# Two GpSimd multiplications in place of a compare and a ScalarE absolute value, in the weight preparation of an attention and two-layer kernel

## The chip, the cores and the metric

The kernel runs on one core of one Trainium2 chip. The time is the device time of one execution in microseconds; the time before is the median of three runs. The profile is of one further execution of the same program.

## The reference

The inputs are q, k, v (4 batches, 8 heads, 576 positions, 64 columns), s (4, 8, 576) and four weight matrices that arrive as float64: `w_in` 512x2048 and `w_out` 2048x512 for each of two layers.

```
scores = q k^T / 8 + min(-(cum_i - cum_j), 0), causal     cum = cumsum(max(s, 0))
attn   = softmax(scores);  x = attn v   -> 2304 tokens x 512
layer 1: h = x @ w_in;  g = h * clip(h + 3, 0, 6) / 6;  x = g @ w_out
layer 2: h = x @ w_in;  g = h * sigmoid(h);             out = g @ w_out
```

All results are float32.

## The kernel before

One core does everything. Each matrix product runs with operands split into a high and a low part (three matmuls for one product), so weights and activations each exist as two fp32r tiles.

**Weights.** A weight chunk is 128 rows of 512 float64 numbers, loaded as 1024 32-bit words per row, so the low and the high words lie alternately, 8 bytes apart. `Chunk` (L130 to L187) makes float32 numbers of them by integer steps. `load` issues the DMA on SP's queue. `fields` (L151 to L164) makes three tiles of words: ScalarE (ACT) scales the low words in place (L159); ACT writes `mag`, the absolute value of the high words, taken as float32, times 2^-112 (L160); GpSimd (POOL) overwrites the high words by the sign bit as an integer, from "less than zero" times -2^31 (L161). `join` puts them together on VectorE (DVE): `mag` shifted left by 3 or'ed with the sign words (L172), plus the low words (L176). Then `high` copies the result as fp32r on ACT (L120) and `low` subtracts on the DVE (L187). The tile `mag` comes from a pool of three, so that a chunk's `mag` can be written when the chunk three before it has been read.

There are 64 chunks: 16 of `i` (from `w_in`) and 16 of `o` (from `w_out`) for each layer. `Feed.tick` runs one step of this line of work: `high` of the chunk two behind, `fields` of the current one, `join` of the one behind, `low` of the chunk two behind, and the load of the chunk three ahead. The first layer's 32 chunks are ticked from the opening on; the second layer's `o` chunks are ticked, and its `i` chunks are made in pairs by `Two` (L887 on), beside the last steps of layer 1 and the first steps of layer 2. `Two.join` calls `fields` for both chunks of a pair and then `join`; `sums` and `split` (L915, L925, L927) make seven combinations of quarters from them, which go through DRAM.

**Order of work.** `slot` (L734 on) writes the order out by hand: in one slot stand one attention head's scores and exponentials, the transposes and the product with v of the head before, at most one step of layer 1 (`first`, `gate_high`, `second`, `gate_low`), and some ticks of the weight feed. Nine slots have no step of layer 1, the others have one. After the heads, layer 1 runs on its last block with the second layer's weights beside it, and then layer 2 (`step2`) on three blocks of 768 tokens. Each engine works through its own stream in order; an instruction that waits holds up all behind it on its engine. Waits are set where tiles are written and read. The framework orders the streams before the run by its own estimate of time.

POOL's other work: memsets of two rows of each new head (L407, L408, before SP loads the head), copies of the gate `g` to `gh` (L114 by `pool_copy`, two scalars, multiply and multiply), the softmax scaling of later heads (L551), the low part of v (L476).

Of the kernel before, what the change touches and what calls it, by code (L numbers as in the profile page):

```python
# [13 lines left out]
AF = mybir.ActivationFunctionType  # L14
ALU = mybir.AluOpType
# [4 lines left out]
SIGN = -(2**31)  # L20


def f32(ap):
    return ap.bitcast(F32)
# [3 lines left out]
def kernel(  # L28
# [15 lines left out]
    nc = tc.nc  # L44
# [43 lines left out]
    def heads_of(x):  # L88
# [8 lines left out]
        out=cmask[:, NZ:], in_=cmask[:, NZ:], pattern=[[-1, P]],  # L97
# [32 lines left out]
    class Chunk:  # L130
# [20 lines left out]
        def fields(self):  # L151

            self.mag = stage.tile([P, DM], I32, tag="mag", name=f"mag{self.nm}")
            if self.src.dtype == F32:
                nc.scalar.copy(f32(self.mag), self.val)
                self.val = f32(self.mag)
                return
            low, high = self.words
            nc.scalar.activation(low, low.bitcast(U32), AF.Copy, scale=2.0**-29)  # L159
            nc.scalar.activation(f32(self.mag), f32(high), AF.Abs, scale=2.0**-112)  # L160
            nc.gpsimd.tensor_scalar(  # L161
                out=high, in0=f32(high), scalar1=0.0, scalar2=float(SIGN),
                op0=ALU.is_lt, op1=ALU.mult,
            )  # L164

        def join(self):
# [166 lines left out]
    def bank(kind, shape, name):  # L333
# [11 lines left out]
        out=srow, in0=srow, scalar1=0.0, scalar2=1.0 / SCALE, op0=ALU.max, op1=ALU.mult  # L345
# [876 lines left out]
```

## Time and profile before

| what | value |
|---|---|
| median of three runs | 1017.48 us (1015.5 to 1018.98) |
| the profiled execution | 1021.31 us, of which span 1019.5 us |
| busy in the span: PE, DVE, ACT, POOL | 97%, 70%, 51%, 33% |
| chain that ended last, by engine | PE 78%, DVE 12%, ACT 3%, DMA 2%, POOL 2%, issue 2% |
| mean granted TensorE clock | 0.991 of full speed |

The page adds up each engine's busy time over one execution. An engine's busy share is a mean over stages: attention with the first layer's weights (to about 150 us), attention with layer 1 (to about 525), the last block of layer 1 with the second layer's weights and the turn to layer 2 (to about 650), layer 2. A DVE or POOL instruction that is held back by another engine while it runs counts as busy all that time. Wait rows name the waiting instruction, its releaser, the sum, the times and the longest.

### The profile page before, as it was taken

How to read it: one execution, taken by the hardware profiler on the slowest of the kernel's cores; microseconds unless marked ns; L12 is line 12 of the kernel's file. 1: busy time of each engine (PE TensorE's matmuls, PEld its weight loads, DVE VectorE, ACT ScalarE, POOL GpSimd, SP SyncE). 2: the span in 40 equal slices, each digit the busy share in tenths (PEclk: the TensorE clock that was granted, in tenths of full speed). 3: DMA queues.
4: the chain of work that ended last, by engine and by line, in shares of the span. 5: the costliest groups of instructions: out<-in, count | busy, mean ns of one | idle time of the engine just before them, and what ended most of it. 6: DMA issues, size and time to landing. Idle time of an engine off the chain costs nothing.

```text
span 1019.5 us, 18411 instructions
## 1 busy us (share of the span) xinstructions
PE 989.4 (97%) x6404; PEld 912.1 (89%) x6404; DVE 715.0 (70%) x1724; ACT 521.3 (51%) x1144; POOL 340.5 (33%) x446
## 2 busy tenths in 40 slices
PE   8988989999999999999999999899999999999997
PEld 5788989999999999999998887789988999888996
DVE  5798998878778888887737799867574334743343
ACT  5798655555556566566526565546353232532232
POOL 7376754453245444444415366423000000000000
PEclk9998999999999999999999999999999999999999
DMA  4686112212312322322114965443354341432411
GB/s 153 197 286 225 38 37 83 74 57 59 91 57 65 92 58 68 94 59 67 59 42 136 380 247 175 146 186 114 145 189 165 132 144 74 177 137 110 145 73 62
DMA packets 52068, 124.80 MB, mean 122 GB/s; under 512 B 10004, under 2 KB 31752, under 8 KB 48648
## 3 DMA queue, kind: packets, MB, share of 16 engines
q1 hardware_dynamic: 51528, 122.97, 35.6%
q8 instruction: 51, 0.84, 0.3%
q10 hardware_dynamic: 448, 0.66, 0.2%
q14 instruction: 41, 0.34, 0.1%
HBM read 98.96 MB, written 24.63 MB: 121 GB/s over the span
## 4 chain that ended last, share of the span: by engine, by line
PE 78%; DVE 12%; ACT 3%; DMA 2%; POOL 2%; issue 2%; DVEq 0%; POOLq 0%; ACTq 0%; SPq 0%
PE a L1029 6%; PE a L1030 6%; PE a L1031 6%; PE h L1013 5%; PE h L1014 5%; PE h L1015 5%; PE acc L300 5%; PE ph L260 5%; PE acc L301 5%; PE acc L299 5%; PE ph L262 5%; PE ph L261 5%; PE poB L617 4%; PE pt0B L567 1%; DVE mago L172 1%
## 5 line engine op out<-in xcount | busy, mean ns | idle before, releaser
L300 PE MATMUL acc<-gl,wo 128*128 128x256 f32 (+1 forms) x512 | 155.0, 304 | 2.7 <-DVE gl L280 2.7
L260 PE MATMUL ph<-xh,wi 128*128 128x256 f32 (+1 forms) x512 | 152.8, 299 | 3.4 <-DVE g L273 3.4
L301 PE MATMUL acc<-gh,wo 128*128 128x256 f32 (+1 forms) x512 | 152.7, 300 | 0.0
L262 PE MATMUL ph<-xh,wi 128*128 128x256 f32 (+1 forms) x512 | 151.3, 296 | 0.6 <-DVE wi L187 0.6
L261 PE MATMUL ph<-xl,wi 128*128 128x256 f32 (+1 forms) x512 | 150.9, 295 | 0.0
L299 PE MATMUL acc<-gh,wo 128*128 128x256 f32 (+1 forms) x512 | 145.2, 301 | 3.1 <-DVE gh L122 3.1
L1071 ACT ACTIVATE gh<-h 128x384 fp32r<-128x384 f32 x96 | 50.3, 524 | 187.7 <-DVE h L1079 187.6
L1029 PE MATMUL a<-wo,gh 128*128 128x512 f32 x288 | 113.5, 394 | 2.6 <-ACT gh L1071 2.5
L1030 PE MATMUL a<-wo,gh 128*128 128x512 f32 x288 | 113.5, 394 | 0.0
L300 PEld LDWEIGHTS acc<-gl,wo 128*128 128x128 f32 x512 | 97.9, 191 | 8.1 <-DVE gl L280 4.9
L260 PEld LDWEIGHTS ph<-xh,wi 128*128 128x128 f32 x512 | 97.0, 190 | 7.1 <-DVE g L273 2.3
L299 PEld LDWEIGHTS acc<-gh,wo 128*128 128x128 f32 x512 | 96.4, 191 | 7.1 <-ACT magi L160 2.5
L301 PEld LDWEIGHTS acc<-gh,wo 128*128 128x128 f32 x512 | 97.9, 191 | 3.6
L262 PEld LDWEIGHTS ph<-xh,wi 128*128 128x128 f32 x512 | 97.0, 189 | 3.8 <-DVE wi L187 0.8
L261 PEld LDWEIGHTS ph<-xl,wi 128*128 128x128 f32 x512 | 96.9, 189 | 2.9
L161 POOL TENSOR_SCALAR rawi<-rawi 128x512 int32<-128x512 f32 x32 | 68.8, 2150 | 76.9 <-ACT magi L160 57.1
L1031 PE MATMUL a<-wo,gl 128*128 128x512 f32 x288 | 90.0, 393 | 0.3 <-DVE gl L1073 0.3
L161 POOL TENSOR_SCALAR rawo<-rawo 128x512 int32<-128x512 f32 x32 | 69.5, 2176 | 44.2 <-ACT mago L160 41.1
L1073 DVE TENSOR_TENSOR gl<-h,gh 128x384 fp32r<-128x384 f32 x96 | 53.6, 558 | 40.7 <-ACT h L1072 39.1
L1079 DVE TENSOR_TENSOR h<-h,u 128x384 f32<-128x384 f32 x72 | 40.1, 557 | 54.8 <-PE h L1015 54.6
L273 DVE SCALAR_TENSOR_TENSOR g<-g,ph 128x512 f32<-128x512 f32 (+1 forms) x76 | 49.5, 652 | 34.5 <-ACT g L272 34.3
L272 ACT ACTIVATE g<-ph,half 128x512 f32<-128x512 f32 (+1 forms) x76 | 50.3, 662 | 37.9 <-PE ph L262 37.2
(232 smaller groups left out, 2655.8 us busy)
## 6 DMA issues: line engine op xcount, KB each, us to landing
w<-w_d SPq DMA_DIRECT2D x18, 1792.0 KB
w_d<-w SPq DMA_DIRECT2D x8, 1792.0 KB
k2B<-in_kT_dram SPq DMA_DIRECT2D x64, 144.0 KB
rawi<-in_w1i_dram SPq DMA_DIRECT2D x16, 512.0 KB
rawo<-in_w1o_dram SPq DMA_DIRECT2D x16, 512.0 KB
rawi<-in_w2i_dram SPq DMA_DIRECT2D x16, 512.0 KB
rawo<-in_w2o_dram SPq DMA_DIRECT2D x16, 512.0 KB
q2B<-in_qT_dram SPq DMA_DIRECT2D x64, 80.0 KB
```

Source lines behind the costliest of these rows:

```text
L161: nc.gpsimd.tensor_scalar(out=high, in0=f32(high), scalar1=0.0, scalar2=float(SIGN), op0=ALU.is_lt, op1=ALU.mult,)
L260: nc.tensor.matmul(o, wih[:, cs], xh[c], start=c == 0, stop=False)
L261: nc.tensor.matmul(o, wih[:, cs], xl[c], start=False, stop=False)
L262: nc.tensor.matmul(o, wil[:, cs], xh[c], start=False, stop=c == NDC - 1)
L299: nc.tensor.matmul(a, woh[:, cs], gh[:, jj, :], start=b0, stop=False)
L300: nc.tensor.matmul(a, woh[:, cs], gl[:, jj, :], start=False, stop=False)
L301: nc.tensor.matmul(a, wol[:, cs], gh[:, jj, :], start=False, stop=b1)
L1013: nc.tensor.matmul(ps, w[:, 0, cs], xh[:, c, :], start=c == 0, stop=False)
L1029: nc.tensor.matmul(accs[t], gh[:, k, cs], woh, start=b0, stop=False)
L1030: nc.tensor.matmul(accs[t], gh[:, k, cs], wol, start=False, stop=False)
L1031: nc.tensor.matmul(accs[t], gl[:, k, cs], woh, start=False, stop=b1)
L1073: nc.vector.tensor_tensor(out=gl[:, i, o], in0=g, in1=f32(gh[:, i, o]), op=ALU.subtract)
```

## The change

In `fields`, ACT's absolute value is gone. POOL makes `mag` as the high words, taken as float32, times 2^-112 and times 1.0, with their sign, and then overwrites the high words, as float32, by themselves times 0.0 and times 1.0: a zero that keeps the sign bit. The shift by 3 in `join` moves the sign bit of `mag` out, so that the or sets it from the sign words as before. The kernel is otherwise the same.

```diff
             nc.scalar.activation(low, low.bitcast(U32), AF.Copy, scale=2.0**-29)
-            nc.scalar.activation(f32(self.mag), f32(high), AF.Abs, scale=2.0**-112)
             nc.gpsimd.tensor_scalar(
-                out=high, in0=f32(high), scalar1=0.0, scalar2=float(SIGN),
-                op0=ALU.is_lt, op1=ALU.mult,
+                out=f32(self.mag), in0=f32(high), scalar1=2.0**-112, scalar2=1.0,
+                op0=ALU.mult, op1=ALU.mult,
+            )
+            nc.gpsimd.tensor_scalar(
+                out=f32(high), in0=f32(high), scalar1=0.0, scalar2=1.0,
+                op0=ALU.mult, op1=ALU.mult,
             )
```

## Rows read from the trace of the kernel before

**Rows 1.** The page: busy us, share of the span and instructions of each engine.
```profile
PE 989.4 (97%) x6404; PEld 912.1 (89%) x6404; DVE 715.0 (70%) x1724; ACT 521.3 (51%) x1144; POOL 340.5 (33%) x446
```

**Rows 2.** Busy us of each engine by stretch (from, to, length; then busy and instructions).
```profile
50.00:150.00 100.00, 88.02 (x676) 84.44 (x675) 94.18 (x236) 74.64 (x176) 69.51 (x54) 0.95 0.46 152
150.00:525.00 375.00, 375.00 (x3098) 371.72 (x3097) 297.61 (x886) 208.35 (x501) 157.82 (x289) 1.00 0.24 70
550.00:650.00 100.00, 95.39 (x408) 76.41 (x407) 89.95 (x136) 60.80 (x101) 59.33 (x35) 0.98 0.69 246
```

**Rows 3.** The same view for line L161 on POOL alone.
```profile
50.00:150.00 100.00, 54.35 (x25) 0.95 0.46 152
550.00:650.00 100.00, 45.36 (x21) 0.98 0.69 246
```

**Rows 4.** Who waited for whom, PE, 50 to 150 us (sum, times, longest).
```profile
PE acc L299 <- DVE gh L122: 3.1, 2, 2.3
```

**Rows 5.** Groups of ACT instructions, whole span (count | busy us, mean ns | idle before).
```profile
L160 ACT ACTIVATE mago<-rawo 128x512 f32<-128x512 f32 x32 | 21.4, 672 | 6.5 <-DVE wo L187 4.9 <-DVE w L927 1.0 <-DVE wi L187 0.5
L120 ACT CAST wo<-mago 128x512 fp32r<-128x512 f32 x32 | 19.9, 620 | 15.9 <-DVE mago L176 15.4 <-DVE sums L545 0.3
```

**Rows 6.** The chain that ended last, in order of time, opening (start us, us).
```profile
24.16 0.66 ACT mago L160
```

**Rows 7.** The same chain at 571 us.
```profile
571.66 0.55 ACT magi L160
572.35 1.98 POOL rawi L161
```

**Rows 8.** Instructions by line on POOL: duration ns, minimum, median, maximum.
```profile
L161 POOL TENSOR_SCALAR rawi<-rawi x32: 1967/2074/2747, 13.6 to 712.1; 128x512 int32<-128x512 f32 x32
L114 POOL TENSOR_SCALAR gh<-g x68: 608/622/1646, 100.0 to 624.7; 128x512 fp32r<-128x512 f32 x68
```

**Rows 9.** Who waited for whom, POOL, whole span.
```profile
POOL rawi L161 <- ACT magi L160: 57.1, 16, 8.6
```

**Rows 10.** Who waited for whom, DVE, 50 to 150 us.
```profile
DVE wi L187 <- ACT wi L120: 1.5, 2, 0.8
...
DVE magi L172 <- POOL rawi L161: 1.2, 1, 1.2
```

**Rows 11.** Timeline of POOL at 100 us (start us, us, instruction).
```profile
100.01 0.62 POOL L114 TENSOR_SCALAR gh<-g 128x512 fp32r<-128x512 f32 x1
100.59 0.84 POOL L114 TENSOR_SCALAR qaA<-q2A 64x256 fp32r<-64x256 f32 x1
101.40 2.00 POOL L161 TENSOR_SCALAR rawo<-rawo 128x512 int32<-128x512 f32 x1
```

**Rows 12.** Timeline of the DVE at 100 us.
```profile
100.08 1.09 DVE L172 SCALAR_TENSOR_TENSOR magi<-magi,rawi 128x512 int32<-128x512 int32 x1 [1.16 <-POOL rawi L161]
101.09 1.50 DVE L187 TENSOR_TENSOR wo<-mago,wo 128x512 fp32r<-128x512 f32 x1
```

**Rows 13.** Timeline of POOL at 60 us.
```profile
60.17 2.02 POOL L161 TENSOR_SCALAR rawi<-rawi 128x512 int32<-128x512 f32 x1 [0.83 <-ACT magi L160]
```

**Rows 14.** Timeline of the DVE at 61 us.
```profile
61.01 0.68 DVE L172 SCALAR_TENSOR_TENSOR mago<-mago,rawo 128x512 int32<-128x512 int32 x1
```

**Rows 15.** Groups of DVE instructions, 50 to 150 us.
```profile
L172 DVE SCALAR_TENSOR_TENSOR magi<-magi,rawi 128x512 int32<-128x512 int32 x13 | 10.5, 808 | 1.2 <-POOL rawi L161 1.2
L187 DVE TENSOR_TENSOR wi<-magi,wi 128x512 fp32r<-128x512 f32 x13 | 10.2, 783 | 1.5 <-ACT wi L120 1.5
L187 DVE TENSOR_TENSOR wo<-mago,wo 128x512 fp32r<-128x512 f32 x13 | 10.0, 771 | 0.0
L172 DVE SCALAR_TENSOR_TENSOR mago<-mago,rawo 128x512 int32<-128x512 int32 x13 | 9.5, 727 | 0.0
L176 DVE CUSTOM_DVE_ANT_0 magi<-rawi,magi 128x1024 uint16<-128x1024 uint16 x13 | 9.1, 703 | 0.1
L176 DVE CUSTOM_DVE_ANT_0 mago<-rawo,mago 128x1024 uint16<-128x1024 uint16 x12 | 9.0, 754 | 0.0
```

## The prediction

> **What bounds the kernel now.** I read the page's busy line first, then the busy time by stage, then who waits for whom in the two stages where TensorE is not full, then single instructions there.
>
> TensorE (PE) is busy 97% of the span [rows 1], so at most some 30 us could go. By stages [rows 2], PE is full from 150 to 525 us and nothing done to GpSimd (POOL) or ScalarE (ACT) there can count; the changed lines don't run there anyway. The open places are 50 to 150 us, where PE is busy 88.0 of 100 us, and 550 to 650 us, where it is busy 95.4 of 100: 12.0 and 4.6 us. In these two stages lie 25 and 21 of the 64 sign instructions of L161 [rows 3], since the weight chunks of the first and the second layer are being made ready. The engine that is nearly full beside PE is VectorE (DVE): 94.2 and 90.0 us of 100. In the first stage the DVE idles 5.8 us in all, and PE's longest stop there is for a DVE copy, 2.3 us [rows 4]. So between 50 and 150 us the in-order stream of the DVE sets the pace: what makes the DVE's work longer delays PE almost one for one, and what makes ACT or POOL quicker helps only where the DVE stands still for them.
>
> **The change part by part.**
>
> *ACT's absolute value (L160) goes.* 64 instructions of 0.67 us, 43 us [rows 5], but on an engine that is not the bound. Off the path this is worth nothing. It is on the path in a few places: once in the opening (24.16 us, 0.66 us, [rows 6]), which I take as 0.7 us gained, and three times between 571 and 593 us, where the chain goes through L160 into L161 (0.55, 0.55 and 0.68 us; [rows 7] is the first of the three, the others, at 581.29 and 592.09, repeat it).
>
> *POOL's compare (L161) becomes two multiplications.* Today one takes, for the chunks of `i`, 1.97 to 2.75 us, median 2.07 [rows 8]; those of `o` differ little. No POOL multiplication over words that lie 8 bytes apart is in the trace. The nearest rows: below, the same two-scalar multiplication over a dense 128x512 tile, median 0.62 us [rows 8]; above, L161 itself, the same strided words under another operation and an integer output, 2.07 us. For ACT the stride costs 0.05 us (0.67 for L160 against 0.62 for the dense cast of the same size, [rows 5]). I therefore stay near the lower end, 0.7 us each, so 1.4 us a chunk for 2.07. Alone this takes about 0.6 us from the latency of a chunk; with L160's share, each of the three places of the chain gets 1.15 to 1.28 us shorter, 3.5 us together.
>
> *The wait moves.* ACT's L160 stood for the chunk to land and for the `mag` tile three chunks back to be read (L187); now the first POOL multiplication stands for both. Behind it on POOL are the memsets of the next head (for which SP's loads wait), the gate copies L114 and the scalings L551. But POOL already stood there for the same events by way of ACT: 57.1 us before the chunks of `i` alone [rows 9]. So I cost this at nothing; if POOL's cover went, it would be the late `gh` copy, one instruction of 0.6 us.
>
> *Where the DVE stands still.* Between 50 and 150 us it waits 1.5 us for ACT (L120 behind L160 in ACT's queue) and 1.2 us for L161 [rows 10]. I let all of it go: 2.7 us.
>
> *What the second POOL instruction does to the DVE.* This is the term that decides. At 100.08 us the DVE instruction L172, which reads two tiles in SBUF, takes 1.09 us; a POOL copy of 0.62 us had started at 100.01. The next, L187, meets the start of two further POOL instructions and takes 1.50 us [rows 11, 12]; left alone, such an instruction takes 0.68 [rows 14]. So the start of a POOL instruction that reads SBUF holds back the DVE's two-tile instruction by about 0.41 us. The sign instruction does the same, but only in its beginning: L161 runs from 60.17 to 62.19, and L172, started 0.84 us into it, takes 0.68 us [rows 13, 14]. What counts is thus the number of POOL instructions, not their length, and the change doubles that number.
>
> The Trainium skill says it otherwise ("SBUF — State Buffer", "Who interferes with whom"): the pair of ports that the two engines share is taken for the whole instruction by whoever comes first, and the other blocks fully. The trace agrees that both are held up, but not with "the whole instruction": by that rule L172 of rows 14 would have waited until 62.19. By it, two instructions of 0.7 us would hold the DVE less than one of 2.07; that result stands among the rivals.
>
> The price of one: the upper end is 0.41 us, at every POOL instruction. The lower end is zero (the DVE happens to be at an instruction that reads PSUM or one tile); a gain is excluded, because the first multiplication starts where the compare did and the dense POOL copy of rows 11 holds the DVE like L161. As a mean: the weight instructions L172, L187 and L176 between 50 and 150 us [rows 15] exceed their usual 0.68 us by 13 x (0.128 + 0.103 + 0.091 + 0.047 + 0.023) + 12 x 0.074 = 6.0 us, over 25 L161 and 7 copies L114 of that size, 0.19 us each. Other two-tile instructions of the DVE are left out of this, so I take 0.25 us.
>
> **The sum.** 50 to 150 us: 25 x 0.25 = 6.3 us more DVE work, less 2.7 us of waits, +3.6. 550 to 650 us: 21 x 0.25 x 0.9 (the DVE's busy share there) = 4.7, less 3.5, +1.2. Opening: -0.7. Together +4.1 us. The profiled execution took 1021.3 us (span 1019.5 and 1.8 around it), 3.8 us above the median of the runs, 1017.5; the difference is added to the median: 1021.6, forecast 1021.5. With the mean stall at 0.41 it is 7.6 + 4.2 - 0.7 = +11.1 us (1028.6); with none, -2.7 - 3.5 - 0.7 = -6.9 us (1010.6). The sum crosses zero at a stall of 6.9 / (25 + 18.9) = 0.16 us. This crossing lies close under my 0.19 to 0.25, which is why the chances are spread.
>
> **Rivals.**
>
> *The shorter chain wins (not slower).* The second POOL instruction starts while the DVE is at work on a PSUM tile or still blocked by the first, so that its own price is under 0.16 us; then the waits for ACT and POOL that go decide. For it: L161 often ran beside L524 and small instructions without loss, as in rows 14. Against: the two follow each other on POOL at once, and in rows 11 and 12 each of three POOL instructions in a row took its share. Time: 1011, at a stall of zero.
> By the rule of the skill, the first figure to change would be the hold of a chunk, 2.07 to 1.4 us, and the gain would be limited only by PE's idle time in both stages, 16.6 us: 1001. Rows 14 speak against it; I give it 2%.
>
> *The stride is what makes L161 slow.* Then each multiplication costs 2.07 us. POOL's 69.5 us between 50 and 150 [rows 2] lose 54.4 [rows 3] and gain 25 x 4.14: 118.6 us of work in 100, +18.6 us; between 550 and 650 it is 100.9, +0.9, and the three places of the chain get 1.6 us longer each, +4.8: in all 24 us, 1041.5. For it: nothing in the trace separates stride from operation on POOL. Against: ACT pays 0.05 us for the same words, and L161 lets go of the DVE early, as if its reading were quick and its arithmetic slow. Between the ends, at 1.2 us each, POOL would be at 75 us of 100 in the first stage and the DVE would still decide: that lies in my range.
>
> *Nothing shows.* Both effects are absorbed: 1017.5. For it: the terms are a few us of opposite sign.
>
> **How the numbers follow.** About 0.3% (3 us) is what a measurement of this kernel can tell from no change. Chances: the forecast 52%, of which 33 end slower and 19 within 0.3%, since +4.1 is little more than 3; the shorter chain 24%, 20 of it faster and 4 within; the skill's rule 2%, faster; the stride 10%, slower; nothing shows 12%, of which 10 within and 2 faster. Faster 24%, within 33%, slower 43%. The range is 1011 to 1029: from a stall of zero to one at every instruction. It leaves out the stride and the skill's rule, and some of the ends. The forecast's own range is 1017 to 1027.
>
> **What would show it.** The two new POOL groups at 0.62 to 0.9 us each where the DVE doesn't hold them; at 2 us the stride is right. L172, L176 and L187 between 50 and 150 us at means some 0.1 us higher, the DVE at over 97 us of that 100, and PE idle there more than 12 us; if the means stay and PE idles less, the shorter chain was right. Between 571 and 593 us, 1.3 to 1.5 us from the landed chunk's turn on POOL to L172. The prediction is wrong if the DVE's means don't rise, or if they do and PE doesn't wait for it.

## The result, and the profile after

The changed kernel takes 1030.35 us (median of four runs, 1029.22 to 1030.71), the kernel before 1018.18 us in the same session (1015.50 to 1018.98). The ratio is 1.0113, 95% interval 1.0090 to 1.0135: slower by 12.2 us, where +4.1 was forecast and 1029 was the end of the range. The profiled execution took 1029.22 us, its span 1027.4.

The diff moves later lines by three: L175, L179 and L190 are L172, L176 and L187 of before, L276 and L283 are L273 and L280, L302 and L303 are L299 and L300. The two GpSimd (POOL) multiplications stand at L160 (`mag`) and L164 (sign).

The page's busy line of the changed kernel (busy us, share of the span, instructions), against [rows 1]:

```profile
PE 989.0 (96%) x6404; PEld 908.9 (88%) x6404; DVE 735.0 (72%) x1724; ACT 486.1 (47%) x1080; POOL 317.0 (31%) x510
```

POOL and ScalarE (ACT) have less to do, and VectorE (DVE), which executes the same 1724 instructions, is busy 20 us longer. By stretch (same columns as [rows 2]):

```profile
50.00:150.00 100.00, 87.55 (x692) 81.62 (x691) 98.49 (x233) 62.26 (x153) 58.92 (x78) 1.00 0.49 149
150.00:525.00 375.00, 374.07 (x3084) 370.96 (x3083) 299.64 (x889) 207.49 (x500) 158.52 (x289) 1.00 0.25 70
550.00:650.00 100.00, 90.40 (x383) 71.61 (x382) 92.73 (x126) 44.48 (x71) 54.16 (x57) 0.97 0.63 230
```

In the first stage the DVE is now full (98.5 of 100 us), but TensorE (PE) is busy as long as before, 87.6 us against 88.0, and does 692 matmuls there for 676. These two rows don't show that nothing was lost there: the granted clock is 1.00 in this execution and was 0.95 in the profile before, which is some 5 us of PE's time (0.05 of 100 us), and 16 matmuls more make up some 2 us of it (an estimate, 0.13 us each). Between 550 and 650 us, at 0.97 and 0.98, PE has lost 5 us and 25 matmuls. So the loss that these rows show lies at the turn to layer 2; what was lost in the first stage is hidden by the clock. The groups of the new POOL instructions, whole span (count | busy us, mean ns | idle before), against [rows 8]:

```profile
L160 POOL TENSOR_SCALAR mago<-rawo 128x512 f32<-128x512 f32 x32 | 30.6, 957 | 41.9 <-DVE wo L190 17.7 <-DMA rawo<-in_w1o_dram 10.1 <-DVE wi L190 7.9
L160 POOL TENSOR_SCALAR magi<-rawi 128x512 f32<-128x512 f32 x32 | 28.3, 887 | 90.8 <-DVE w L930 41.6 <-DVE wo L190 23.0 <-DMA rawi<-in_w1i_dram 11.8
L164 POOL TENSOR_SCALAR rawo<-rawo 128x512 f32<-128x512 f32 x32 | 28.3, 885 | 2.1
L164 POOL TENSOR_SCALAR rawi<-rawi 128x512 f32<-128x512 f32 x32 | 26.9, 843 | 2.0
```

The stride costs little: the means are under 1 us, for 2.07 us of the compare, and where nothing holds it a multiplication takes 0.65 us. Of the DVE's weight groups of the first stage, `mago` at L175 went from 727 to 890 ns and L179 from 754 to 849, while `magi` at L175 fell from 808 to 734 ([rows 15]); these are the rows that changed most:

```profile
L175 DVE SCALAR_TENSOR_TENSOR mago<-mago,rawo 128x512 int32<-128x512 int32 x13 | 11.6, 890 | 0.0
L179 DVE CUSTOM_DVE_ANT_0 mago<-rawo,mago 128x1024 uint16<-128x1024 uint16 x13 | 11.0, 849 | 0.0
L175 DVE SCALAR_TENSOR_TENSOR magi<-magi,rawi 128x512 int32<-128x512 int32 x12 | 8.8, 734 | 0.0
```

PE's longest stop lies at the turn. Who waited for whom, PE, 500 to 660 us (sum, times, longest), and POOL's timeline ahead of that stop:

```profile
PE acc L302 <- POOL gh L114: 6.3, 1, 6.3
```

```profile
629.61 1.02 POOL L160 TENSOR_SCALAR mago<-rawo 128x512 f32<-128x512 f32 x1 [2.42 <-DVE wo L190]
630.72 0.96 POOL L164 TENSOR_SCALAR rawo<-rawo 128x512 f32<-128x512 f32 x1
631.64 1.08 POOL L160 TENSOR_SCALAR mago<-rawo 128x512 f32<-128x512 f32 x1
632.80 0.97 POOL L164 TENSOR_SCALAR rawo<-rawo 128x512 f32<-128x512 f32 x1
633.74 0.64 POOL L160 TENSOR_SCALAR mago<-rawo 128x512 f32<-128x512 f32 x1
634.46 0.96 POOL L164 TENSOR_SCALAR rawo<-rawo 128x512 f32<-128x512 f32 x1
635.38 1.05 POOL L114 TENSOR_SCALAR gh<-g 128x512 fp32r<-128x512 f32 x1
```

Three chunks of layer 2 stand in POOL's stream right ahead of the last gate copy of layer 1, and PE waits 6.3 us for it. In the kernel before one chunk stands there, and PE doesn't wait for the copy:

```profile
622.63 2.08 POOL L161 TENSOR_SCALAR rawo<-rawo 128x512 int32<-128x512 f32 x1 [0.32 <-ACT mago L160]
624.67 1.07 POOL L114 TENSOR_SCALAR gh<-g 128x512 fp32r<-128x512 f32 x1
```

The source does not ask for the difference, the framework's ordering of the streams made it. The prediction had no term for that. So two causes are to be told apart: the instructions themselves, and the order in which the framework put everything else once they had changed.

How the two engines hold each other is seen in single instructions. POOL and then the DVE of the changed kernel at 82 us:

```profile
82.04 0.65 POOL L164 TENSOR_SCALAR rawi<-rawi 128x512 f32<-128x512 f32 x1
83.31 0.65 POOL L160 TENSOR_SCALAR mago<-rawo 128x512 f32<-128x512 f32 x1 [0.62 <-DVE wi L190]
```

```profile
82.10 1.13 DVE L190 TENSOR_TENSOR wi<-magi,wi 128x512 fp32r<-128x512 f32 x1
83.49 1.01 DVE L179 CUSTOM_DVE_ANT_0 mago<-rawo,mago 128x1024 uint16<-128x1024 uint16 x1
```

POOL's first multiplication ends at 82.69 and the DVE's instruction at 83.23, 0.54 us later; the second pair ends at 83.96 and 84.50, again 0.54 apart. Left alone such a DVE instruction takes 0.68 us, of which some 0.1 lies beside its predecessor. So the DVE instruction does its work when the multiplication has ended, whenever that began: it is held for the whole rest of it. Of the 57 two-tile instructions of the DVE over 512 words that start during one of the new multiplications in this trace, 55 end 0.53 to 0.62 us after it. The same two views of the kernel before, at the compare:

```profile
57.31 2.02 POOL L161 TENSOR_SCALAR rawo<-rawo 128x512 int32<-128x512 f32 x1 [1.35 <-DMA q2A<-in_qT_dram]
```

```profile
57.34 1.18 DVE L172 SCALAR_TENSOR_TENSOR magi<-magi,rawi 128x512 int32<-128x512 int32 x1
58.45 0.68 DVE L187 TENSOR_TENSOR wo<-mago,wo 128x512 fp32r<-128x512 f32 x1
```

L172 ends at 58.52; less 0.54 it was let go at 57.98, 0.67 us into the compare, which ran on to 59.33 without holding L187. Over the whole trace of the kernel before, of 20 such DVE instructions that start in the first 0.64 us of a compare 16 take 1.02 to 1.18 us, which by the same working puts their release 0.65 to 1.10 us after its start; of the 57 that start later two are held. A compare of 2.02 us and a multiplication of 0.65 us thus hold the DVE for times of the same order. The Trainium skill's rule ("SBUF — State Buffer", "Who interferes with whom"), that the shared ports are taken for the whole instruction, agrees with the multiplications (0.54 us after their end) and not with the compare (released 0.9 to 1.4 us ahead of its end).

### The profile page after: what moved, and what is told of

It is laid out like the page before. It is cut to its first block, busy times and chain, and to the rows that moved or that the text cites. A ratio compares the mean times of both kernels' runs of the same rounds, so it can differ in the third digit from the quotient of the medians.

```text
span 1027.4 us, 18445 instructions
## 1 busy us (share of the span) xinstructions
PE 989.0 (96%) x6404; PEld 908.9 (88%) x6404; DVE 735.0 (72%) x1724; ACT 486.1 (47%) x1080; POOL 317.0 (31%) x510
## 4 chain that ended last, share of the span: by engine, by line
PE 71%; DVE 13%; DMA 5%; POOL 4%; issue 3%; SPq 2%; ACT 1%; POOLq 0%; DVEq 0%; ACTq 0%
PE a L1032 6%; PE a L1034 6%; PE a L1033 6%; PE h L1016 5%; PE h L1017 5%; PE h L1018 5%; PE ph L263 4%; PE acc L302 4%; PE ph L264 4%; PE ph L265 4%; PE acc L304 4%; PE acc L303 4%; PE poB L620 4%; DMA rawi<-in_w2i_dram 2%; PE pt0B L570 1%
## 5 line engine op out<-in xcount | busy, mean ns | idle before, releaser
L303 PE MATMUL acc<-gl,wo 128*128 128x256 f32 (+1 forms) x512 | 154.4, 303 | 5.1 <-DVE gl L283 5.0
L302 PE MATMUL acc<-gh,wo 128*128 128x256 f32 (+1 forms) x512 | 145.7, 301 | 6.7 <-POOL gh L114 6.6
L303 PEld LDWEIGHTS acc<-gl,wo 128*128 128x128 f32 x512 | 97.0, 189 | 12.1 <-DVE gl L283 8.7
L302 PEld LDWEIGHTS acc<-gh,wo 128*128 128x128 f32 x512 | 96.0, 190 | 11.5 <-POOL gh L114 7.4
L114 POOL TENSOR_SCALAR gh<-g 128x512 fp32r<-128x512 f32 x68 | 49.2, 723 | 81.1 <-DVE g L276 74.2
L276 DVE SCALAR_TENSOR_TENSOR g<-g,ph 128x512 f32<-128x512 f32 (+1 forms) x76 | 49.5, 652 | 33.8 <-ACT g L275 33.8
L1016 PE MATMUL h<-x0t,w 128*128 128x384 f32 x192 | 65.2, 340 | 1.1 <-DVE u L1082 0.6
```

Source lines behind the costliest of these rows:

```text
L302: nc.tensor.matmul(a, woh[:, cs], gh[:, jj, :], start=b0, stop=False)
L303: nc.tensor.matmul(a, woh[:, cs], gl[:, jj, :], start=False, stop=False)
L1016: nc.tensor.matmul(ps, w[:, 0, cs], xh[:, c, :], start=c == 0, stop=False)
```

## The experiments

In the first four runs the framework orders the streams. In all others every engine's stream is written down instruction by instruction, as ordering edges without semaphores, so that only the instructions of the weight words differ. "In before's order" means the streams of the kernel before, a new POOL instruction standing right beside L161's place. The kernel before was run beside each group; its medians were 1018.62, 1019.24, 1019.56 and 1018.13 us.

### The sign half alone, and a second instruction behind it

```diff
-                out=high, in0=f32(high), scalar1=0.0, scalar2=float(SIGN),
-                op0=ALU.is_lt, op1=ALU.mult,
+                out=f32(high), in0=f32(high), scalar1=0.0, scalar2=1.0,
+                op0=ALU.mult, op1=ALU.mult,
```

> ScalarE's absolute value stays; only the sign words are made by one multiplication by 0.0. As many GpSimd instructions as before, but shorter. If the stalls of VectorE under the second GpSimd instruction made the change slow (theory: stalls), this runs at 1014 to 1019 us, with L172, L176 and L187 between 50 and 150 us at the means of before (0.70 to 0.81 us). If the changed order of the streams did it (theory: order), it is slow too: here the last gate copy of layer 1 stands behind 14 word instructions of the o chunks on GpSimd, as against 11 before and 16 in the changed kernel, so 1023 to 1028 us, with a stop of TensorE of some us for that copy near 630 us.

Measured: 1028.18 us (1025.85 to 1031.27), ratio 1.0092 (1.0067 to 1.0117). The number of POOL instructions is that of before, each is shorter, and still most of the loss is there (9.6 of 12.2 us). PE's wait for a gate copy at the turn is 2.2 us in it. By the forecast's term nothing should have been lost.

The second kernel adds a multiplication of the sign words by 1.0:

```diff
+            nc.gpsimd.tensor_scalar(
+                out=f32(high), in0=f32(high), scalar1=1.0, scalar2=1.0,
+                op0=ALU.mult, op1=ALU.mult,
+            )
```

> As the kernel with only the sign multiplication, plus a second GpSimd multiplication of the sign words by 1.0, which changes no value: two GpSimd instructions a chunk with ScalarE's absolute value kept. Stalls: 4 to 9 us slower than the one-multiplication kernel, VectorE's busy time up by some 13 us. Order: within 3 us of it, whatever VectorE's busy time does.

Measured: 1033.82 us (1032.34 to 1035.48), ratio 1.0146 (1.0129 to 1.0163), 5.6 us above the one before. In both the framework chose the order anew, so these two did not separate the causes.

### Layer 2's weight work queued behind layer 1's gate

```diff
-                pair(q)
+                behind_gate(pair, q)
...
-                twos[q].split()
+                behind_gate(twos[q].split)
...
-            outs2(t - NF // 2 + 1)
+            behind_gate(outs2, t - NF // 2 + 1)
```

`behind_gate` makes what it issues on the DVE and POOL stand behind the latest gate instruction of layer 1. The edit was made to the changed kernel and to the kernel before.

> The changed kernel, with the second layer's weight work (pairs and o chunks) queued behind the latest layer-1 gate on VectorE and GpSimd, in issue order only, without a wait. Order: the stop of TensorE of 6.3 us for the last gate copy goes, and with it the low clock behind it; 1020 to 1024 us. Stalls: the order costs little, 1027 to 1031 us.

> The kernel before with the same queueing. It shows what the queueing does by itself. Both theories: 1015 to 1020 us; if it costs more than 3 us, the weights come too late for layer 2, and the same cost is in the changed kernel with the queueing.

Measured: 1028.13 us (1026.70 to 1032.34), ratio 1.0085 (1.0068 to 1.0102); the kernel before with the same edit 1019.73 us, ratio 1.0006 (0.9991 to 1.0020). The stop of 6.3 us is gone from the changed kernel, and 2.2 us came back, which the intervals don't separate. Some 9.5 us are still lost without the stop (against 1018.62), so it was a place where the time showed, and not the cause of most of it.

### The same instructions, in either order

```diff
         tile_attention_moe_moe_kernel(tc, *args)
+        in_order(tc)
```

> The changed kernel's instructions, each engine's stream in exactly the order of the kernel before (the new GpSimd multiplication for mag right ahead of the sign word's), pinned in issue order without waits. Order theory: the time of before, 1016 to 1021 us. Stalls theory: the slow-down stays, 1022 us (the prediction's +4.1) to 1030 us.

> The reverse: the instructions of before (ScalarE's absolute value, GpSimd's compare) in the order that the changed kernel has on every engine. Order theory: as slow as the changed kernel or slower, 1026 to 1034 us. Stalls theory: near before, 1016 to 1022 us.

> One multiplication for the sign words in place of the compare, all else and every stream's order as before. Order theory: the 9.6 us that this edit cost in its own order go, and the shorter GpSimd instruction can gain a little: 1012 to 1019 us. If the multiplication holds VectorE longer than the compare does, it stays above 1021 us.

> A second GpSimd multiplication of the sign words by 1.0, in the order of before: against the one-multiplication kernel in the same order this is the price of one more GpSimd instruction a chunk and nothing else. Stalls theory: 4 to 10 us slower than it. Order theory: within 3 us of it.

| instructions | framework's own order | in before's order | in the changed kernel's order |
|---|---|---|---|
| before | 1018 to 1019.6 | the same | 1039.04, ratio 1.0202 (1.0165 to 1.0238) |
| changed | 1030.35, 1.0113 (1.0090 to 1.0135) | 1027.90, 1.0078 (1.0041 to 1.0116) | the same |
| sign half | 1028.18, 1.0092 (1.0067 to 1.0117) | 1016.74, 0.9981 (0.9959 to 1.0002) | |
| sign half, second instruction | 1033.82, 1.0146 (1.0129 to 1.0163) | 1031.25, 1.0126 (1.0083 to 1.0168) | |

Instructions and order both count. The order alone makes the sign half 11.4 us slower, and the kernel before 20 us slower when it is run in the order that the framework made for the other instructions. In that run PE's stop at the turn is there too (same view, 500 to 660 us):

```profile
PE acc L299 <- POOL gh L114: 7.8, 2, 7.2
```

For the changed kernel the order is the smaller part: in before's order it still loses 8.7 us (1027.90 against 1019.24), and its own order adds 2.4 by the times, or 3.5 by the two ratios, which the intervals don't separate. In one order the second multiplication costs 14.5 us (1031.25 against 1016.74).

These times are not holds alone. The 70 executions of the kernel before that ran beside the variants took 1014.7 to 1026.1 us, and the slower ones had the lower mean granted clock: 0.8 us more for each 0.001 less (correlation -0.84). Their mean is 0.993; the changed kernel's four are at 0.993 too, but the sign half in its own order is at 0.987 and the one with the second multiplication in before's order at 0.989. By that slope 5 to 6 of the 11.4 us and some 3 of the 14.5 go with the clock. This is an estimate, and whether PE's pauses lower the clock or the lower clock comes first isn't shown by it.

### The other half, and no POOL instruction at all

```diff
-            nc.scalar.activation(f32(self.mag), f32(high), AF.Abs, scale=2.0**-112)
+            nc.gpsimd.tensor_scalar(
+                out=f32(self.mag), in0=f32(high), scalar1=2.0**-112, scalar2=1.0,
+                op0=ALU.mult, op1=ALU.mult,
+            )
```

> The other half of the change: GpSimd makes the exponent words by a multiplication, ScalarE's absolute value is gone, and the compare of before stays; every engine's stream is that of before. If the two halves add up, this costs what both cost together in this order (1027.9) less what the sign half gained (1016.7 against 1018.6): 1029 to 1031 us. If GpSimd's own time per chunk matters (2.07 and 0.65 us in place of 0.65 and 0.65), GpSimd is at about 86 us of 100 between 50 and 150 us and the chunks come later: 1034 us and more. If the second instruction costs only where it follows another multiplication, it is near 1019.

Measured: 1032.20 us (1030.17 to 1034.33), ratio 1.0125 (1.0096 to 1.0154), a little above what adding the halves gave.

```diff
-            nc.gpsimd.tensor_scalar(
-                out=high, in0=f32(high), scalar1=0.0, scalar2=float(SIGN),
-                op0=ALU.is_lt, op1=ALU.mult,
-            )
+            nc.scalar.activation(f32(high), f32(high), AF.Copy, scale=0.0)
```

> No GpSimd instruction per chunk at all: ScalarE makes the sign words too, as a third activation with the scale 0.0, behind the absolute value; streams as in before. If each GpSimd instruction that reads SBUF holds up VectorE, the excess of VectorE's instructions over their unhindered times falls from 9 and 11 us (first 150 us, and 500 to 725 us) to about 2 and 5, and the time goes to 1008 to 1012 us. The rival: ScalarE, at 75 us of 100 between 50 and 150 us, gets 25 x 0.68 = 17 us more, so that VectorE waits for its casts and exponentials, and the time is 1020 us or more although the excess has fallen. (The zero may lose its sign in this activation; then the words are off and only the time counts.)

Its words come out wrong (that the zero loses its sign there isn't shown), so only its time counts. Measured: 1030.81 us (1028.70 to 1032.04), ratio 1.0109 (1.0083 to 1.0136): the rival held. The windows row of 50 to 150 us (columns as in [rows 2]), then PE's longest wait for ACT and the DVE's waits for ACT's weight copies, up to 150 us:

```profile
50.00:150.00 100.00, 87.01 (x638) 81.50 (x638) 84.24 (x238) 91.02 (x208) 16.42 (x27) 0.93 0.48 146
```

```profile
PE acc L296 <- ACT magi L160: 3.1, 1, 3.1
```

```profile
DVE wo L184 <- ACT wo L120: 3.6, 4, 2.5
DVE wi L184 <- ACT wi L120: 3.6, 4, 1.6
```

With nearly the same work (238 instructions, 236 before) the DVE falls from 94.2 to 84.2 us of 100, so the holds by POOL were worth about 10 us of DVE time there already before. But ACT goes to 91 us, and PE and the DVE wait for it instead; the granted clock is down to 0.93 there, and its mean over the four executions, 0.984, goes with some 8 of the 11 us by the slope above. Here the freed DVE time was worth nothing, since another engine was late.

### Number, length, or chain

The sign half in before's order, and behind it POOL multiplications into a tile that nobody reads, so that they stand in no chunk's chain: over 64 words, over 256, and twice over 256. Alone they take 0.24 and 0.41 us, for 0.65 over 512 words; the tile is float32 for 64 words and uint8 for 256 (instructions by line, duration ns, minimum, median, maximum):

```profile
L166 POOL TENSOR_SCALAR scratch<-rawi x32: 244/356/765, 14.3 to 712.9; 128x64 f32<-128x64 f32 x32
L166 POOL TENSOR_SCALAR scratch<-rawi x32: 410/528/932, 14.3 to 712.6; 128x256 uint8<-128x256 f32 x32
```

```diff
+            nc.gpsimd.tensor_scalar(
+                out=scratch, in0=f32(high)[:, :64], scalar1=1.0, scalar2=1.0,
+                op0=ALU.mult, op1=ALU.mult,
+            )
```

> One GpSimd multiplication for the sign words, and behind it a second one over only 64 of the 512 words per row, into a tile that nobody reads: it holds GpSimd briefly and stands in no chunk's chain. Streams as in before. Against the same without it (1016.7) a second instruction of full length in the chain cost 14.5 us. If the number of instructions counts and not their length: +10 us or more, 1027 and up. If the length counts: an eighth, +2 us, 1018.5. If the cost is that the chunk's words come later to VectorE: under +1 us, 1017 to 1018.

> As the kernel with 64 words, but the second instruction goes over 256 of the 512 words per row, again into a tile that nobody reads. If the number counts: the same +10 us or more as with 64 words. If the length counts: half of 14.5, 1024. If the cost is that the chunk's words come later: 1017 to 1018.5, since GpSimd only frees itself 0.3 us later.

> The sign words by one multiplication, and behind it two further GpSimd multiplications over 256 words per row each, into a tile that nobody reads: the full length of the second instruction that cost 14.5 us, but outside the chunk's chain, and three instructions per chunk. One half cost 3.3 us (1020.0 against 1016.7). If the hold of VectorE by length sets the price: 1023 to 1031 us (twice the half's 3.3 at the least). If the 14.5 us came from the chunk's chain: about 1020 to 1021.

Measured: 1017.82 us with 64 words (ratio 0.9986, 0.9964 to 1.0008), 1020.00 with 256 (1.0002, 0.9981 to 1.0022), 1028.87 with twice 256 (1.0094, 1.0065 to 1.0122). Against 1016.74 (1016.93 in the last session) that is +1.1, +3.3 and +11.9 us; by the ratios, since the first two ran on another chip than the sign half, +0.5, +2.1 and +11.6. The count of instructions does not set the price: a short one per chunk is nearly free, and the intervals don't separate it from none. Nor does the chain set most of it: outside it twice 0.41 us costs 11.9 us, for 14.5 inside it with 0.65. The price grows with length, and faster than in proportion. A part of that excess goes with TensorE's clock: the mean is 0.987 with twice 256 words and 0.993 with 256, some 5 us by the slope above, as much as 11.9 exceeds twice 3.3. It is seen in the opening. PE of 20 to 50 us (from, to, length; PE's busy us and instructions, weight loads, DVE, ACT, POOL; granted clock, share of DMA, GB/s), without the second instruction and with it in the chain:

```profile
20.00:50.00 30.00, 26.45 (x186) 21.26 (x184) 22.72 (x87) 22.44 (x64) 3.61 (x6) 1.00 0.63 186
```

```profile
20.00:50.00 30.00, 27.13 (x157) 21.27 (x156) 19.54 (x74) 18.58 (x55) 3.92 (x6) 0.83 0.66 192
```

PE is no less busy and gets 29 matmuls less done: the granted clock is at its lower level, 1.2 GHz, for part of the stretch. Layer 1's first matmul starts 4.5 us later (44.3 against 39.8 us), and in the run with twice 256 words at 44.1. Not all of that need belong to the variant: in a second profile of the kernel without the second instruction the clock of this stretch is 0.94 and that matmul starts at 41.7. What made the clock fall there these runs don't show.

### The change in one layer at a time

```diff
+            if self.key[1] == 0:
...
+            else:
```

with the changed instructions in the first branch and those of before in the second (`== 1` in the other kernel); before's order.

> The change for the 32 chunks of layer 1 alone; the chunks of layer 2 as in before; every stream in the order of before. With both layers changed this order took 1027.9 us against 1018.6. In the traces VectorE's excess over unhindered times rose by 5.6 us in the first 150 us and by 11.4 us between 500 and 725 us. If the excess sets the price and ScalarE's relief is spread evenly, this kernel loses little: 1018 to 1021 us. By the forecast's own terms (+3.6 - 0.7) it would be about 1021.5 and the other layer the cheaper one; if the rise is all in the first stage, 1027.

> The change for the 32 chunks of layer 2 alone; those of layer 1 as in before; streams in the order of before. If VectorE's excess at the turn sets the price: 1024 to 1028 us. By the forecast's term for this stage (+1.2): 1020. If the rise is all in the first stage: 1018 to 1019.

Measured: layer 1's chunks changed, 1021.34 us (1018.13 to 1024.45), ratio 1.0028 (1.0011 to 1.0044); layer 2's, 1025.23 us (1022.99 to 1027.25), ratio 1.0059 (1.0035 to 1.0082). So +3.2 and +7.1 us, together 10.3, about the 8.7 of both within their intervals. The DVE's busy us of 0 to 150 and of 525 to 650 us (from, to, length; busy and instructions; granted clock, DMA share, GB/s): first of before, then with layer 1 changed, then with layer 2 changed.

```profile
0.00:150.00 150.00, 126.40 (x347) 0.95 0.50 158
525.00:650.00 125.00, 100.95 (x155) 0.99 0.60 213
```

```profile
0.00:150.00 150.00, 133.32 (x348) 0.98 0.51 158
525.00:650.00 125.00, 101.44 (x156) 1.00 0.61 216
```

```profile
0.00:150.00 150.00, 125.85 (x347) 0.95 0.50 158
525.00:650.00 125.00, 106.01 (x147) 1.00 0.57 203
```

Each kernel changes its own stage and leaves the other alone. Summed over the DVE's instructions, the time above what the same line takes unhindered rises from 11.8 to 18.1 us up to 150 us with layer 1 changed, and from 10.3 to 21.8 us between 500 and 725 us with layer 2 changed: +6.3 and +11.5. (By what is taken as unhindered these rises come out at 6 to 7 and 10 to 12.) Not all of it is lost, since waits come back. The DVE's longest one for POOL, 500 to 650 us, of before and with layer 2 changed:

```profile
DVE magi L172 <- POOL rawi L161: 5.5, 2, 3.5
```

```profile
DVE magi L182 <- POOL rawi L165: 1.3, 1, 1.3
```

What reaches PE is seen in its own waits, 500 to 725 us, again of before and with layer 2 changed; for POOL it waits in neither:

```profile
PE acc L300 <- DVE gl L280: 1.0, 3, 0.4
```

```profile
PE acc L310 <- DVE gl L290: 3.8, 4, 2.1
```

PE's stream is the same in both kernels: its matmul that starts at 600.1 us before starts 0.1 us later with layer 2 changed, and the one at 650.0 us 4.6 us later. So the loss lies between 600 and 650 us, and PE's waits for the DVE grow (all together from 1.3 to 5.1 us), not its waits for POOL. The two profiled executions, with the same mean clock (0.991), differ by 4.4 us (spans 1023.9 and 1019.5); of the 7.1 us of the medians some 1.5 go with the clock (0.9915 on average). For layer 1 the two profiles can't show the price: the one with it changed is the fastest of ten executions, and PE is 0.9 us ahead of before's at 150 us, where before's had lost some 3 us more to the clock (0.95 and 0.98, rounded, in the rows above). There the 3.2 us rest on the medians.

How the hold adds up where POOL's instructions stand in a row is seen in the same kernel at 582 us, POOL and then the DVE (L161 and L165 are the two multiplications, L182, L186 and L290 before's L172, L176 and L280):

```profile
582.98 0.65 POOL L161 TENSOR_SCALAR magi<-rawi 128x512 f32<-128x512 f32 x1
583.71 0.98 POOL L165 TENSOR_SCALAR rawi<-rawi 128x512 f32<-128x512 f32 x1
584.65 1.10 POOL L161 TENSOR_SCALAR mago<-rawo 128x512 f32<-128x512 f32 x1
```

```profile
583.05 1.12 DVE L290 TENSOR_TENSOR gl<-g,gh 128x512 fp32r<-128x512 f32 x1 [0.52 <-POOL gh L114]
584.10 1.14 DVE L186 CUSTOM_DVE_ANT_0 magi<-rawi,magi 128x1024 uint16<-128x1024 uint16 x1
```

The engines go in turn: POOL to 583.63, the DVE to 584.17, POOL to 584.69, the DVE to 585.24. Each finishes 0.52 to 0.55 us after the other let go, and each pays for the other. A GpSimd instruction as long that reads nothing from SBUF was not run; it would tell the hold from GpSimd's own time in every stage.

### Does the sign half alone beat the kernel before?

> The sign words by one multiplication, ScalarE's absolute value kept, streams in the order of before: the same program that took 1016.7 us, 0.19% under before with an interval from 0.9959 to 1.0002. A second measurement with more rounds: if the gain is real, the ratio stays near 0.998 and its interval ends under 1; if not, it comes to 0.999 to 1.001.

Measured: 1016.93 us (1014.80 to 1021.97, 12 runs), ratio 0.9980 (0.9963 to 0.9996). With one multiplication in place of the compare, ScalarE's absolute value kept and the streams held in before's order, the kernel is 0.2% faster than before, just clear of no change.

## Why the prediction was wrong

**The step that failed** is the term for 550 to 650 us: "21 x 0.25 x 0.9 (the DVE's busy share there) = 4.7, less 3.5, +1.2". Layer 2's chunks alone cost 7.1 us in before's order, in the place where PE came to wait for the DVE. Both parts of the term were off. The holds came to 11.5 us for 32 chunks, 0.36 a chunk and not 0.25, and they reach beyond the 100 us that were counted. And the three places of the chain [rows 7] didn't get 1.15 to 1.28 us shorter each, because POOL is held by the DVE as the DVE is by POOL. The chain of the changed kernel where it goes through such a chunk (start us, us):

```profile
566.14 1.68 POOL magi L160
567.89 0.67 POOL rawi L164
568.59 0.70 DVE magi L175
```

From POOL's start to its end it is 2.42 us, for 2.66 before (571.66 to 574.33, ACT and POOL). The gain is 0.24 us where 1.2 was forecast: the first multiplication took 1.68 us, since a DVE instruction of 1.23 us had started 0.06 us ahead of it. The next two such places of the chain take 1.89 us (579.03 to 580.92) and 3.18, for 2.69 and 2.75 before; the last of them is

```profile
586.84 1.37 POOL mago L160
588.30 1.72 POOL rawo L164
```

Together some 0.6 us came back where the term had 3.5.

**Right in its sum, in part by luck:** the first stage. The forecast for it and the opening was 6.3 - 2.7 - 0.7 = +2.9 us; layer 1's chunks alone cost 3.2 (1.1 to 4.5 by the interval of the ratio), and the DVE's holds rose by the 6.3 us of the forecast. But that was 0.20 us for each of 32 chunks up to 150 us, and the forecast had 0.25 for 25 chunks from 50 us on: two errors that cancel. That a second POOL instruction costs time with everything else in its place is shown by the runs in one order; that it takes it by way of the DVE is seen at the turn, in PE's waits, and argued from the holds in the first stage. The signs named for it came in part: the DVE at over 97 us (98.5), PE idle more than 12 us (12.4, which at 12.0 before says little); but the three weight lines' mean rose by only 0.03 us, from 0.76 to 0.79, and other two-tile instructions took a part of the holds (L283 from 619 to 696 ns).

**Right for a wrong reason:** "what counts is thus the number of POOL instructions, not their length". The number told the price here only since every word instruction over 512 words, compare or multiplication, holds the DVE for a like time, a multiplication for its 0.65 us. The runs with 64 and 256 words show that length does count. The lines that the prediction read show the hold to the end already: the copy of rows 11 ends at 100.63 us, and L172 of rows 12 at 101.17, 0.54 later. The 0.41 us taken as the upper end of one hold stood close to the 0.45 us by which the 1.13 us of L190 exceeds its 0.68.

**Missing:** that an edit of two instructions changes the framework's order of everything. "The kernel is otherwise the same", as the section on the change has it, is true of the source and not of the streams. For the changed kernel this is 2.4 to 3.5 us of the 12.2, not separated from zero; for the sign half alone it is 11.4 us, shown. The sum has no term for TensorE's clock either, which is lower in several variants, though not in the changed kernel.

The sum with the measured terms: 3.2 + 7.1 = 10.3 us, where both layers together measured 8.7, and 2.4 to 3.5 for the order: 11.1 to 13.8 for the 12.2 measured. Of the rivals, the stride falls (0.65 us a multiplication), and so do the shorter chain and no effect at all. The Trainium skill's rule forecast 1001 because it let the compare hold the DVE for 2.07 us; the compare holds it for its first 0.65 to 1.10 us, no longer than two multiplications do, so that there was nothing to win.

It stays open why the change adds 0.36 us of holds to a chunk of layer 2 and 0.20 to one of layer 1, what lowers the clock in some variants, and which of the framework's many shifts made the sign half slower in its own order.

## What to carry to other kernels

Between a GpSimd instruction that reads SBUF and a VectorE instruction with two SBUF inputs, add up the time for which either holds the other, per instruction, and do it in the stage where VectorE is late: work moved from ScalarE to GpSimd is paid for by VectorE, and GpSimd pays too. When a framework orders the streams by its own estimates, compare the order of the two programs before reading the time of an edit, and run the edit in the old order as well. Read the granted clock beside each time, and take no price from a single profile of either kernel.

## What the runs showed that was not expected

- A GpSimd compare into int32 over 128x512 words takes 2.0 us and holds VectorE only in its first 0.65 to 1.10 us; a multiplication takes 0.65 us and holds it to its end.
- The order of the streams, with the same instructions, moved this kernel by 11.4 us (sign half) and by 20 us (kernel before).
- A third ScalarE activation per chunk in place of the GpSimd instruction took the holds away (VectorE 94.2 to 84.2 us of 100) and made the kernel 1.1% slower.
- In the profiles of two variants PE was 4 us behind at the end of the opening with a granted clock of 0.83 of full speed from 20 to 50 us, although it was as busy as without.
- The times of the kernel before go with the mean granted clock of the execution: 0.8 us for each 0.001, over 70 executions.
